# Attention on one core: P of half the units transposed by DMA instead of TensorE, scores run further ahead

## The chip, the cores and the metric

The kernel runs on one core of one Trainium2 chip. Such a core has TensorE (PE; matmuls and their weight loads, PEld), VectorE (DVE), ScalarE (ACT), GpSimd (POOL), and SyncE (SP), which here only issues DMAs; sixteen DMA engines serve all queues. The metric is the device time of one execution in microseconds (us), lower is better. The kernel before takes 1212.79 us, the median of three runs (1212.4 to 1214.84).

## The reference

Two attention problems of the same shape, A and B, with their own inputs; their outputs stand side by side.

```python
B, Sq, D = 16, 144, 448          # x: (B, Sq, D), bfloat16
H, Sk, Dh = 16, 512, 256         # k_cache, v_cache: (B, H, Sk, Dh)
q = (x @ wq).reshape(B, Sq, H, Dh).transpose(0, 2, 1, 3)
scores = einsum("bhqd,bhkd->bhqk", q, k_cache) * Dh ** -0.5
p = softmax(scores, axis=-1)
o = einsum("bhqk,bhkd->bhqd", p, v_cache)
out = o.transpose(0, 2, 1, 3).reshape(B, Sq, H * Dh) @ wo
```

In problem B the reference repeats K and V over head groups, but there are as many of them as heads, so nothing is repeated.

## The kernel before, in words

**Units.** One unit U is one (problem, batch, head): 2 x 16 x 16 = 512 units in one long sequence. The 144 query rows of a unit are split into 112 rows (part A, one unit at a time) and 32 rows (part B, four units stacked to 128 rows).

**One pass of the loop** (variable i, one iteration per unit) emits the steps of several units, each ahead of PV by its own lead:

- Q of unit i+15 (`t_q`, L314: 8 matmuls into the one bank qp_ps) and its copy to qt_sb (`t_evac_q`; VectorE L326 or ScalarE L330).
- every eighth iteration the scores of part B of eight units (`t_sb`, L342).
- scores of part A of unit i+5 (`t_sa`, L418: 2 matmuls into one of two banks sa_ps), the row maximum (VectorE, L429), exp into a slot of pa_sb (ScalarE, L440), and one iteration later the reciprocal (L450) and the multiplication by it on POOL (`t_norm`, L458).
- the transpose of the normalized P of unit i+2 (`t_ta`, L471: 4 transposes by TensorE, 112 x 128 each, back into a bank of sa_ps) and its copy to pt_sb (`t_evac_pta`, VectorE, L481). Keys are taken with a stride: chunk c holds keys 4p+c, as V lies in SBUF with four neighbouring keys per partition. So the transposes read pa_sb with a step of four.
- twice in eight iterations the same for part B (`t_tb`, L394, and L403).
- PV of unit i (`t_pv`, L504: 8 matmuls of V against the transposed P) and its copy to the ring (ScalarE, L519 and L521).
- usually one piece of the output projection (`t_op_piece`, L542: 2 matmuls against wo), from a queue of finished 128-row chunks; stores go out on POOL's queue (`t_store`, L571).

**Loads.** All loads are issued on SyncE's queue in one fixed order: K of eight units as one transposing DMA out of HBM (`t_load_k`, L290, 2 MB), V of four units (`t_load_v`, L299, 1 MB), x of four batches (two transposing DMAs, L280 and L281), wq in four pieces (L259, L261) and wo in eight (L269). The list `dma_plan` is sorted by deadline; an entry is emitted once i has come within a lead of the deadline and its slot's last reader has been emitted. K and V have three slots each (NK, NV), x three (NXG).

**Order and waits.** Each engine's program is written in the order in which the loop emits it. The class `_Sched` keeps, for each buffer slot, who wrote and read it, and puts semaphore waits ahead of an instruction (also of a DMA's issue) where its data or its slot come from another engine. An instruction whose wait isn't met holds everything behind it on its engine; a DMA's issue that waits holds SyncE's later issues. Slot counts that matter: pa_sb 5 (NPA), pt_sb 8 (NPT), qt_sb 12 (NQT).

Of the kernel before, what the change touches and what calls it, by code (L numbers as in the profile page):

```python
# [7 lines left out]
AF = mybir.ActivationFunctionType  # L8
# [4 lines left out]
PE, ACT, DVE, POOL, SP = "pe", "act", "dve", "pool", "sp"  # L13
# [109 lines left out]
def bass_concat_heads__mha_block_cached__gqa_block_cached__near_ridge_kernel(  # L123
# [18 lines left out]
    NP = 2  # L142
    Bn, SQ, D = A_x.shape
# [14 lines left out]
    NWG = NWO // WOG  # L158
    NPC = NWO // OPP

    LQ, LS, LT = 15, 5, 2
    LSB = 7
    NK, NV, NXG = 3, 3, 3
    XB = 4 if Bn % 4 == 0 else (2 if Bn % 2 == 0 else 1)
    NQT, NPA, NPB, NPT, NST, NSTB, NOST = 12, 5, 2, 8, 4, 2, 3
    RS = 4
    RC = RS * 128
    OP_DELAY = 2
# [6 lines left out]
    with contextlib.ExitStack() as es:  # L175
# [33 lines left out]
            sem_names.append("v%d" % i)  # L209
        for i in range(NXG):  # L210
            sem_names.append("xt%d" % i)
        for i in range(HG):
            sem_names.append("wq%d" % i)
        for i in range(NWG):
# [219 lines left out]
        def t_exp(U):  # L434
            bank = U % 2
            sl = U % NST
            psl = U % NPA

            def e(a):
                return a.activation(pa_sb[0:QA, psl, :], sa_ps[bank][0:QA, :], AF.Exp,  # L440
                                    bias=stat[0:QA, NEG + sl:NEG + sl + 1], scale=1.0,
                                    accum_out=stat[0:QA, RSUM + sl:RSUM + sl + 1])
            S.add(ACT, e, reads=[(("sap", bank), ("s", U)), (("neg", sl), U)],
                  writes=[(("pa", psl), (U, 0)), (("rsum", sl), U)], banks=["sa%d" % bank], name="ex%d" % U)
# [17 lines left out]

        def t_ta(U):
            psl = U % NPA
            bank = U % 2

            def e(t):
                src = pa_sb[0:QA, psl, :].rearrange("q (p c) -> q c p", c=4)
                ins = None
                for c in range(4):  # L470
                    ins = t.transpose(pta_ps[bank][:, c * 128:c * 128 + QA], src[:, c, :], ident[0:QA, 0:QA])  # L471
                return ins
            S.add(PE, e, reads=[(("pa", psl), (U, 1)), ("ident", 0)], writes=[(("sap", bank), ("t", U))],
                  banks=["sa%d" % bank], name="TA%d" % U)

        def t_evac_pta(U):
            sl = U % NPT
            bank = U % 2

            def e(v):  # L480
                return v.tensor_copy(pt_sb[:, sl, :, 0:QA],  # L481
                                     pta_ps[bank][:, 0:512].rearrange("p (c q) -> p c q", c=4)[:, :, 0:QA])
            S.add(DVE, e, reads=[(("sap", bank), ("t", U))], writes=[(("pta", sl), U)], banks=["sa%d" % bank],
                  name="epta%d" % U)
# [93 lines left out]
        t_ident()  # L578
        dma_plan = []

        def plan(lo, deadline, lead, fn, *args):
            dma_plan.append((deadline, len(dma_plan), lo, lead, fn, args))

        s_min = -LQ - 24
        for XG in range(NXGT):
            pr, j = divmod(XG, Bn // XB)
            u_first = pr * NU + j * XB * H
            dl = u_first - LQ
            if XG >= NXG:
                pr0, j0 = divmod(XG - NXG, Bn // XB)  # L590
                lo = pr0 * NU + (j0 + 1) * XB * H - 1 - LQ + 1
            else:
                lo = s_min
            plan(lo, dl, 40, t_load_x, XG)
        for pr in range(NP):
            for hg in range(HG):
                dl = pr * NU + 4 * hg - LQ
                lo = pr * NU - H + 4 * hg + 3 - LQ + 1 if pr > 0 else s_min
                plan(lo, dl, 10 ** 6, t_load_wq, pr, hg)
        for wg in range(NWG):  # L600
            plan(s_min, H - 4 + 2 * wg, 10 ** 6, t_load_wo, 0, wg)
        for SG in range(NSG):
            dl = 8 * SG - LSB
            lo = 8 * (SG - NK) + 7 - LS + 1 if SG >= NK else s_min
            plan(lo, dl, 12, t_load_k, SG)
        for G in range(NG):
            dl = 4 * G
            lo = 4 * (G - NV) + 3 + 1 if G >= NV else s_min
            plan(lo, dl, 8, t_load_v, G)
        dma_plan.sort(key=lambda t: t[:2])  # L610
        _prev = s_min
        _tmp = []
        for dl, sq, lo, lead, fn, args in dma_plan:
            _prev = max(_prev, lo, dl - lead)
            _tmp.append((_prev, dl, sq, fn, args))
        dma_plan = _tmp

        u_tail0 = NT - H
        pr_l, b_l, _h = unit(NT - 1)
# [32 lines left out]
        while True:  # L652
            while dma_plan and dma_plan[0][0] <= i:
                _sl, _dl, _sq, fn, args = dma_plan.pop(0)
                fn(*args)
            sgi, ph = divmod(i + LSB, 8)
            do_sb = ph == 0 and 0 <= sgi < NSG
            ga, gb = 2 * sgi, 2 * sgi + 1
            ok = 0 <= sgi < NSG
            if ok and ph == 1:  # L660
                t_exp_b(ga)
            if ok and ph == 3:
                t_exp_b(gb)
            if ok and ph == 2:
                t_recip_b(ga)
                t_norm_b(ga)
            if ok and ph == 4:
                t_recip_b(gb)
                t_norm_b(gb)
            while stores and stores[0][1] <= i:  # L670
                t_store(stores.pop(0)[0])
            if do_sb and sgi == 0:
                t_sb(sgi)
            u = i + LQ
            if 0 <= u < NT:
                t_q(u)
                t_evac_q(u)
            if do_sb and sgi > 0:
                t_sb(sgi)
            u = i + LS  # L680
            if 0 <= u < NT:
                t_sa(u)
                t_max(u)
                t_exp(u)
            u = i + LS - 1
            if 0 <= u < NT:
                t_recip(u)
                t_norm(u)
            u = i + LT
            if 0 <= u < NT:  # L690
                t_ta(u)
                t_evac_pta(u)
            if ok and ph == 3:
                t_tb(ga)
                t_evac_ptb(ga)
            if ok and ph == 7:
                t_tb(gb)
                t_evac_ptb(gb)
            if ok and ph == 0:
                t_max_b(ga)  # L700
            if ok and ph == 2:
                t_max_b(gb)
            u = i
            if 0 <= u < NT:
                t_pv(u)
                t_evac_ot(u)
                pr, b, h = unit(u)
                if u >= u_tail0:
                    for r in tail_chunks:
                        if h == 0:  # L710
                            op_first[r], op_last[r] = 0, NWO - 1
                        for dc in range(2):
                            fifo[tail_bank[r]].append((r, 2 * h + dc, i + 1))
                if h == H - 1:
                    g_end = pr * RP + (b + 1) * SQ
                    lo = (pr * RP + b * SQ) // 128
                    for r in range(lo, (g_end - 1) // 128 + 1):
                        r_end = min((r + 1) * 128, pr * RP + Bn * SQ)
                        if g_end >= r_end and r not in tail_bank:
                            queue_chunk(r, i + OP_DELAY)  # L720
            if i >= 0:
                credit += OP_RATE
            if i >= u_tail0 - 14:
                credit += 4.0
            if i >= NT:
                credit += 4 * OPP
            for bank in ("op", "qp"):
                while fifo[bank] and fifo[bank][0][2] <= i and credit >= 1 and (bank == "qp" or i >= op_hold):
                    r, cs = pop_items(bank, i, OPP)
                    credit -= len(cs)  # L730
                    t_op_piece(r, cs, bank)
                    pr = r // NCH
                    if r == last_chunk_of[pr] and pr + 1 < NP:
                        for c in cs:
                            if c % WOG == WOG - 1:
                                t_load_wo(pr + 1, c // WOG)
                    if cs[-1] == op_last[r]:
                        t_evac_op(r, bank, ACT if bank == "op" else DVE)
                        stores.append((r, i + (2 if i < NT else 0)))
                        if bank == "op":  # L740
                            op_hold = i + 2
            if not fifo["op"] and not fifo["qp"]:
                credit = min(credit, 2.0 * OPP)
            i += 1
            if i >= NT and not fifo["op"] and not fifo["qp"] and not dma_plan and not stores:
                break
# [54 lines left out]
```

## Time and profile before

| what | value |
| --- | --- |
| runs | 1212.79 us median (1212.4 to 1214.84) |
| span of the profiled execution | 1210.9 us, 33868 instructions |
| TensorE, weight loads | 97% and 75% of the span |
| VectorE, ScalarE, POOL | 64%, 62%, 56% |
| transposes of part A on TensorE, L471 | 2048 matmuls, 186.5 us busy, mean 213 ns |
| their copies, L481 | 512, 190.5 us busy, mean 372 ns |
| chain that ended last | TensorE 90% (L471: 8%), DMA 6%, VectorE 2% |
| HBM read, written | 148.90 MB, 4.13 MB |
| K load, issue to landing (median) | 15.0 us for A, 15.1 us for B |
| V load, issue to landing (median) | 6.0 and 6.1 us |
| SyncE waiting for TensorE at V's issues (L299 for L542) | 235.3 us in 59 waits |

The profile is one execution. Busy time of TensorE overlaps itself, since a matmul starts before the one ahead of it has ended: distances between starts show what a step costs. SyncE's rows are issues: the time in a row is how long the queue was held, and landing comes later. A stretch's DMA share is the packets' time over sixteen engines, which can be over 1 where packets overlap.

### The profile page before, as it was taken

The numbers are of one execution on the slowest core, as the hardware profiler recorded it, in microseconds if no ns is written. First come the engines' busy times: TensorE is split into PE (matmuls) and PEld (weight loads), VectorE is DVE, ScalarE is ACT, GpSimd is POOL, SyncE is SP. The second block draws the span as 40 slices with busy tenths as digits, with TensorE's granted clock in tenths as the row PEclk, the third lists the DMA queues.
The fourth block names the chain that finished last, engine by engine and source line by source line (L and its number), as shares of the span: only waits on it lengthen the run. The fifth ranks groups of instructions, "written<-read, shape, count | busy, mean of one in ns | idle before, by whom it ended". The sixth has DMA issues, their size and how long they took to land.

```text
span 1210.9 us, 33868 instructions
## 1 busy us (share of the span) xinstructions
PE 1176.6 (97%) x13952; PEld 902.6 (75%) x13952; DVE 770.1 (64%) x2179; ACT 753.9 (62%) x2213; POOL 679.6 (56%) x682
## 2 busy tenths in 40 slices
PE   4998999999999999999999999999999999999997
PEld 3676777777777777777777777777877777777765
DVE  1765666666666666666566666666666666666563
ACT  1655666666666666666566666666666666666553
POOL 0654565565555565565555655655655655655553
PEclk9999999999999999999999999999999999999999
DMA  9999999999999999999999999999999999999971
GB/s 250 296 269 290 246 255 225 242 251 246 245 238 234 228 263 231 239 239 233 278 284 272 278 272 267 247 257 224 245 245 236 226 245 244 244 239 243 223 178 47
DMA packets 627033, 294.15 MB, mean 243 GB/s; under 512 B 548416, under 2 KB 556608, under 8 KB 626880
## 3 DMA queue, kind: packets, MB, share of 16 engines
q1 hardware_dynamic: 625152, 287.85, 102.2%
q0 software_dynamic: 1728, 4.13, 1.2%
q8 instruction: 111, 1.82, 0.6%
q14 instruction: 42, 0.34, 0.1%
HBM read 148.90 MB, written 4.13 MB: 126 GB/s over the span
## 4 chain that ended last, share of the span: by engine, by line
PE 90%; DMA 6%; DVE 2%; SPq 1%; ACT 0%; issue 0%; POOL 0%; ACTq 0%
PE qp_ps L314 20%; PE ot_ps L504 19%; PE sa_ps L418 18%; PE op_ps L542 17%; PE sa_ps L471 8%; PE sb_ps L342 5%; DMA kt_sb<-in_A_k_cache_dram 4%; PE sb_ps L394 2%; DMA kt_sb<-in_B_k_cache_dram 1%; DVE stat L429 1%; DMA wq_sb<-in_A_wq_dram 0%; PE qp_ps L542 0%; SPq L280 0%; DVE qt_sb L326 0%; DVE pt_sb L481 0%
## 5 line engine op out<-in xcount | busy, mean ns | idle before, releaser
L458 POOL TENSOR_TENSOR pa_sb<-pa_sb,stat 112x512 bf16<-112x512 bf16 x512 | 532.7, 1041 | 491.6 <-DVE stat L450 491.4
L440 ACT ACTIVATE pa_sb<-sa_ps,stat 112x512 bf16<-112x512 f32 x512 | 352.0, 688 | 409.6 <-DVE stat L429 408.6
L429 DVE TENSOR_REDUCE stat<-sa_ps 112x1 f32<-112x512 f32 x512 | 353.9, 691 | 324.7 <-PE sa_ps L418 321.4
L314 PEld LDWEIGHTS qp_ps<-xt_sb,wq_sb 128*128 128x128 bf16 x4096 | 290.5, 99 | 93.1 <-issue 11.3
L314 PE MATMUL qp_ps<-xt_sb,wq_sb 128*128 128x144 bf16 x4096 | 344.1, 228 | 16.1 <-DMA wq_sb<-in_A_wq_dram 10.3
L504 PE MATMUL ot_ps<-pt_sb,v_sb 128*128 128x144 bf16 x4096 | 340.9, 226 | 0.0
L418 PE MATMUL sa_ps<-kt_sb,qt_sb 128*112 128x512 bf16 x1024 | 311.1, 385 | 1.0 <-DVE pt_sb L481 0.8
L542 PE MATMUL op_ps<-wo_sb,ring 128*128 128x448 bf16 x1120 | 279.6, 353 | 0.0
L504 PEld LDWEIGHTS ot_ps<-pt_sb,v_sb 128*128 128x128 bf16 x4096 | 269.1, 98 | 0.4
L471 PEld LDWEIGHTS sa_ps<-ident,pa_sb 112*128 112x128 bf16 x2048 | 161.2, 114 | 104.9 <-ACT pa_sb L440 24.8
L519 ACT ACTIVATE ring<-ot_ps 128x288 bf16<-128x288 f32 (+8 forms) x512 | 190.3, 372 | 4.5 <-PE ot_ps L504 4.5
L481 DVE COPY pt_sb<-sa_ps 128x448 bf16<-128x448 bf16 x512 | 190.5, 372 | 2.4 <-PE sa_ps L471 2.4
L471 PE MATMUL sa_ps<-ident,pa_sb 112*128 112x112 bf16 x2048 | 186.5, 213 | 0.1
L326 DVE TENSOR_SCALAR qt_sb<-qp_ps 128x288 bf16<-128x288 f32 x256 | 117.0, 457 | 98.2 <-PE qp_ps L314 97.5
L382 POOL TENSOR_TENSOR pb_sb<-pb_sb,stat 128x512 bf16<-128x512 bf16 x128 | 133.1, 1040 | 27.1 <-DVE stat L374 27.1
L330 ACT ACTIVATE qt_sb<-qp_ps 128x288 bf16<-128x288 f32 x256 | 106.0, 414 | 35.1 <-PE qp_ps L314 33.4
L418 PEld LDWEIGHTS sa_ps<-kt_sb,qt_sb 128*112 128x112 bf16 x1024 | 96.9, 129 | 38.5 <-issue 26.8
L542 PEld LDWEIGHTS op_ps<-wo_sb,ring 128*128 128x128 bf16 x1120 | 95.5, 98 | 28.1 <-issue 0.9
L440 ACT ACTIVATION_READ_ACCUMULATOR pa_sb<-sa_ps,stat 112x1 f32 x512 | 98.9, 193 | 0.0
L354 DVE TENSOR_REDUCE stat<-sb_ps 128x1 f32<-128x512 f32 x128 | 87.1, 680 | 3.6 <-PE sb_ps L342 3.6
L364 ACT ACTIVATE pb_sb<-sb_ps,stat 128x512 bf16<-128x512 f32 x128 | 88.5, 691 | 0.0
L450 DVE RECIPROCAL stat<-stat 112x1 f32<-112x1 f32 x512 | 78.4, 153 | 0.5 <-ACT pa_sb L440 0.5
(23 smaller groups left out, 368.4 us busy)
## 6 DMA issues: line engine op xcount, KB each, us to landing
v_sb<-in_A_v_cache_dram SPq DMA_DIRECT2D x64, 1024.0 KB, 6.0
v_sb<-in_B_v_cache_dram SPq DMA_DIRECT2D x64, 1024.0 KB, 6.1
out_dram<-ost_sb POOLq DMA_DIRECT2D x36, 112.0 KB, 5.1
wo_sb<-in_A_wo_dram SPq DMA_DIRECT2D x8, 448.0 KB, 7.4
wo_sb<-in_B_wo_dram SPq DMA_DIRECT2D x8, 448.0 KB, 5.7
wq_sb<-in_A_wq_dram SPq DMA_DIRECT2D x4, 768.0 KB, 6.2
wq_sb<-in_B_wq_dram SPq DMA_DIRECT2D x4, 768.0 KB, 7.8
wq_sb<-in_A_wq_dram SPq DMA_DIRECT2D x4, 128.0 KB, 6.6
```

The lines of the kernel that those rows point to most:

```text
L314: ins = t.matmul(qp_ps[:, dc * SQ:(dc + 1) * SQ], lhsT=wq_sb[:, kc, c0:c0 + 128], rhs=xt_sb[:, xsl, kc, xo:xo + SQ], start=(kc == 0 and dc ...
L326: return v.tensor_scalar(qt_sb[:, sl, :, :], src, 1.0 / 16.0, None, op0=ALU.mult)
L382: return g.tensor_tensor(pb_sb[:, psl, :], pb_sb[:, psl, :], stat[:, RINVB + sl:RINVB + sl + 1].to_broadcast([128, SK]), op=ALU.mult)
L418: ins = t.matmul(sa_ps[bank][0:QA, :], lhsT=qt_sb[:, U % NQT, dc, 0:QA], rhs=kt_sb[:, ksl, dc, ko:ko + SK], start=(dc == 0), stop=(dc == 1))
L429: return v.tensor_reduce(stat[0:QA, NEG + sl:NEG + sl + 1], sa_ps[bank][0:QA, :], axis=AX.X, op=ALU.max, negate=True)
L440: return a.activation(pa_sb[0:QA, psl, :], sa_ps[bank][0:QA, :], AF.Exp, bias=stat[0:QA, NEG + sl:NEG + sl + 1], scale=1.0, accum_out=stat ...
L458: return g.tensor_tensor(pa_sb[0:QA, psl, :], pa_sb[0:QA, psl, :], stat[0:QA, RINV + sl:RINV + sl + 1].to_broadcast([QA, SK]), op=ALU.mult)
L471: ins = t.transpose(pta_ps[bank][:, c * 128:c * 128 + QA], src[:, c, :], ident[0:QA, 0:QA])
L481: return v.tensor_copy(pt_sb[:, sl, :, 0:QA], pta_ps[bank][:, 0:512].rearrange("p (c q) -> p c q", c=4)[:, :, 0:QA])
L504: ins = t.matmul(ot_ps[ob][:, dc * SQ:(dc + 1) * SQ], lhsT=v_sb[:, vsl, j, c * DH + dc * 128:c * DH + (dc + 1) * 128], rhs=pt_sb[:, sl, c, ...
L519: ins = a.activation(ring[:, 2 * h:2 * h + 2, c0:c0 + n1], src[:, :, 0:n1], AF.Copy)
L542: ins = t.matmul(acc[0:m, 0:D], lhsT=ring[:, c, col0:col0 + m], rhs=wo_sb[:, c, :], start=(c == first), stop=(c == last))
```

## The change

1. P of units U with U % 8 < 4 is transposed by a DMA out of SBUF (`t_dma_pt`), one for four units: source 112 rows x 2048 columns of pa_sb, destination four neighbouring slots of pt_sb. It is issued on SyncE in the order of the loads, planned at i = U0 - 4 for the four units U0 to U0+3. `t_ta` and `t_evac_pta` of those units are left out; the other four of every eight keep them.
2. Scores of part A (with maximum, exp, normalization) run 12 units ahead of PV instead of 5 (LS); pa_sb has 12 slots instead of 5.
3. Exp writes pa_sb with the keys already grouped by chunk: it reads PSUM with a step of four and writes in order, so a unit's 512 columns are four blocks of 128. `t_ta` reads them in order.
4. The bank of `t_ta` becomes (U+1) % 2, as the lead of the scores went from odd to even.
5. `dma_plan` is ordered by hand: each load has an iteration and a rank among those of the same iteration (wq 0, x and the new DMA 1, K 2, V 3, wo 4). K is planned at 8 SG - 28, V at 4 G - 8.
6. x has two slots instead of three (NXG); two semaphores (pt0, pt1) are added.

```diff
--- before.py
+++ after.py
@@ -158,11 +158,11 @@
     NWG = NWO // WOG
     NPC = NWO // OPP
 
-    LQ, LS, LT = 15, 5, 2
+    LQ, LS, LT = 15, 12, 2
     LSB = 7
-    NK, NV, NXG = 3, 3, 3
+    NK, NV, NXG = 3, 3, 2
     XB = 4 if Bn % 4 == 0 else (2 if Bn % 2 == 0 else 1)
-    NQT, NPA, NPB, NPT, NST, NSTB, NOST = 12, 5, 2, 8, 4, 2, 3
+    NQT, NPA, NPB, NPT, NST, NSTB, NOST = 12, 12, 2, 8, 4, 2, 3
     RS = 4
     RC = RS * 128
     OP_DELAY = 2
@@ -209,6 +209,8 @@
             sem_names.append("v%d" % i)
         for i in range(NXG):
             sem_names.append("xt%d" % i)
+        for i in range(2):
+            sem_names.append("pt%d" % i)
         for i in range(HG):
             sem_names.append("wq%d" % i)
         for i in range(NWG):
@@ -437,7 +439,8 @@
             psl = U % NPA
 
             def e(a):
-                return a.activation(pa_sb[0:QA, psl, :], sa_ps[bank][0:QA, :], AF.Exp,
+                return a.activation(pa_sb[0:QA, psl, :].rearrange("q (c p) -> q c p", c=4),
+                                    sa_ps[bank][0:QA, :].rearrange("q (p c) -> q c p", c=4), AF.Exp,
                                     bias=stat[0:QA, NEG + sl:NEG + sl + 1], scale=1.0,
                                     accum_out=stat[0:QA, RSUM + sl:RSUM + sl + 1])
             S.add(ACT, e, reads=[(("sap", bank), ("s", U)), (("neg", sl), U)],
@@ -462,10 +465,10 @@
 
         def t_ta(U):
             psl = U % NPA
-            bank = U % 2
+            bank = (U + 1) % 2
 
             def e(t):
-                src = pa_sb[0:QA, psl, :].rearrange("q (p c) -> q c p", c=4)
+                src = pa_sb[0:QA, psl, :].rearrange("q (c p) -> q c p", c=4)
                 ins = None
                 for c in range(4):
                     ins = t.transpose(pta_ps[bank][:, c * 128:c * 128 + QA], src[:, c, :], ident[0:QA, 0:QA])
@@ -473,9 +476,23 @@
             S.add(PE, e, reads=[(("pa", psl), (U, 1)), ("ident", 0)], writes=[(("sap", bank), ("t", U))],
                   banks=["sa%d" % bank], name="TA%d" % U)
 
+        def by_dma(U):
+            return U % 8 < 4
+
+        def t_dma_pt(U0):
+            ps0, ts0 = U0 % NPA, U0 % NPT
+            sem = "pt%d" % ((U0 // 8) % 2)
+
+            def e(q):
+                return q.dma_start_transpose(
+                    pt_sb[:, ts0:ts0 + 4, :, :].rearrange("p s c q -> p (s c) q")[:, :, 0:QA],
+                    pa_sb[0:QA, ps0:ps0 + 4, :].rearrange("q s k -> q (s k)")).then_inc(sems[sem], 16)
+            S.add(SP, e, reads=[(("pa", (U0 + j) % NPA), (U0 + j, 1)) for j in range(4)],
+                  writes=[(("pta", (U0 + j) % NPT), U0 + j) for j in range(4)], dma_sem=sem, name="DT%d" % U0)
+
         def t_evac_pta(U):
             sl = U % NPT
-            bank = U % 2
+            bank = (U + 1) % 2
 
             def e(v):
                 return v.tensor_copy(pt_sb[:, sl, :, 0:QA],
@@ -578,42 +595,29 @@
         t_ident()
         dma_plan = []
 
-        def plan(lo, deadline, lead, fn, *args):
-            dma_plan.append((deadline, len(dma_plan), lo, lead, fn, args))
+        def plan(t, prio, fn, *args):
+            dma_plan.append((t, prio, len(dma_plan), fn, args))
 
         s_min = -LQ - 24
         for XG in range(NXGT):
             pr, j = divmod(XG, Bn // XB)
             u_first = pr * NU + j * XB * H
-            dl = u_first - LQ
-            if XG >= NXG:
-                pr0, j0 = divmod(XG - NXG, Bn // XB)
-                lo = pr0 * NU + (j0 + 1) * XB * H - 1 - LQ + 1
-            else:
-                lo = s_min
-            plan(lo, dl, 40, t_load_x, XG)
-        for pr in range(NP):
-            for hg in range(HG):
-                dl = pr * NU + 4 * hg - LQ
-                lo = pr * NU - H + 4 * hg + 3 - LQ + 1 if pr > 0 else s_min
-                plan(lo, dl, 10 ** 6, t_load_wq, pr, hg)
+            lo = u_first - XB * H - LQ + 4 if XG >= NXG else s_min
+            plan(max(lo, u_first - LQ - 40), 1, t_load_x, XG)
+        for hg in range(HG):
+            plan((-32, -29, -26, -21)[hg], 0, t_load_wq, 0, hg)
+            for pr in range(1, NP):
+                plan(pr * NU - H + 4 * hg + 3 - LQ + 1, 0, t_load_wq, pr, hg)
         for wg in range(NWG):
-            plan(s_min, H - 4 + 2 * wg, 10 ** 6, t_load_wo, 0, wg)
+            plan(H - 18 + 2 * wg, 4, t_load_wo, 0, wg)
         for SG in range(NSG):
-            dl = 8 * SG - LSB
-            lo = 8 * (SG - NK) + 7 - LS + 1 if SG >= NK else s_min
-            plan(lo, dl, 12, t_load_k, SG)
+            plan(8 * SG - 28, 2, t_load_k, SG)
         for G in range(NG):
-            dl = 4 * G
-            lo = 4 * (G - NV) + 3 + 1 if G >= NV else s_min
-            plan(lo, dl, 8, t_load_v, G)
-        dma_plan.sort(key=lambda t: t[:2])
-        _prev = s_min
-        _tmp = []
-        for dl, sq, lo, lead, fn, args in dma_plan:
-            _prev = max(_prev, lo, dl - lead)
-            _tmp.append((_prev, dl, sq, fn, args))
-        dma_plan = _tmp
+            plan(4 * G - 8, 3, t_load_v, G)
+        for U0 in range(0, NT, 8):
+            plan(U0 - 4, 1, t_dma_pt, U0)
+        dma_plan.sort(key=lambda t: t[:3])
+        dma_plan = [(t, p, n, fn, args) for t, p, n, fn, args in dma_plan]
 
         u_tail0 = NT - H
         pr_l, b_l, _h = unit(NT - 1)
@@ -687,7 +691,7 @@
                 t_recip(u)
                 t_norm(u)
             u = i + LT
-            if 0 <= u < NT:
+            if 0 <= u < NT and not by_dma(u):
                 t_ta(u)
                 t_evac_pta(u)
             if ok and ph == 3:
```

## Prediction

> **What bounds the kernel now.** I read the engine shares first.
>
> ```profile
> PE 1176.6 (97%) x13952; PEld 902.6 (75%) x13952; DVE 770.1 (64%) x2179; ACT 753.9 (62%) x2213; POOL 679.6 (56%) x682
> ...
> DMA  9999999999999999999999999999999999999971
> ...
> q1 hardware_dynamic: 625152, 287.85, 102.2%
> ```
>
> TensorE leads, but the DMA engines show nine tenths in nearly every slice: two candidates stand close together. The PE timeline in a settled stretch (start, length, line) prices the removed step.
>
> ```profile
> 601.06 0.66 PE L314 MATMUL qp_ps<-xt_sb,wq_sb 128*128 128x144 bf16 x8
> 601.56 0.59 PE L418 MATMUL sa_ps<-kt_sb,qt_sb 128*112 128x512 bf16 x2
> 602.00 0.36 PE L471 MATMUL sa_ps<-ident,pa_sb 112*128 112x112 bf16 x4
> 602.19 0.67 PE L504 MATMUL ot_ps<-pt_sb,v_sb 128*128 128x144 bf16 x8
> 602.70 0.54 PE L542 MATMUL op_ps<-wo_sb,ring 128*128 128x448 bf16 x2
> 603.07 0.66 PE L314 MATMUL qp_ps<-xt_sb,wq_sb 128*128 128x144 bf16 x8
> ```
>
> Lengths overlap; starts don't. Four transposes move the next start by 602.19 - 602.00 = 0.19 us, of a 2.01 us iteration. Next, how full the DMA engines are, by stretch; the last two figures of a row are the DMA share and GB/s.
>
> ```profile
> 38.00:125.00 87.00, 80.80 (x989) 61.41 (x986) 55.81 (x160) 53.33 (x151) 48.73 (x48) 1.00 1.17 279
> 125.00:550.00 425.00, 424.69 (x5111) 327.37 (x5109) 281.26 (x798) 275.14 (x812) 247.77 (x247) 1.00 1.04 242
> 550.00:720.00 170.00, 167.17 (x1986) 129.10 (x1984) 109.81 (x312) 108.19 (x329) 97.07 (x97) 0.99 1.16 274
> 720.00:1150.00 430.00, 429.87 (x5150) 333.31 (x5148) 282.45 (x803) 278.04 (x816) 251.14 (x250) 1.00 1.06 241
> ...
> 388.00:392.00 4.00, 4.00 (x45) 2.88 (x43) 3.34 (x10) 3.66 (x12) 3.03 (x4) 1.00 1.27 290
> 384.00:386.00 2.00, 2.00 (x30) 1.06 (x27) 0.62 (x2) 1.45 (x4) 1.04 (x1) 1.00 1.01 353
> ```
>
> While K streams (388 to 392, a transpose) the engines deliver 290 GB/s at share 1.27; while V streams (384 to 386) 353 at 1.01. Each is full at its own figure; a full mix shows 1.16 to 1.17, as in the first 125 us and around the change of problem (550 to 720). Elsewhere 1.04 and 1.06 leave spare time: 425 x (1 - 1.04/1.165) = 46 us and 430 x (1 - 1.06/1.165) = 39 us, together 85 us. That is all the room a new transfer has before 1150. Last, SyncE's queue where it is fed without a wait.
>
> ```profile
> 93.70 15.29 SPq L290 DMA_TRANSPOSE kt_sb<-in_A_k_cache_dram  x1
> 109.03 1.13 SPq L299 DMA_DIRECT2D v_sb<-in_A_v_cache_dram  x2
> 110.21 14.96 SPq L290 DMA_TRANSPOSE kt_sb<-in_A_k_cache_dram  x1
> ...
> 605.57 15.41 SPq L290 DMA_TRANSPOSE kt_sb<-in_B_k_cache_dram  x1
> 621.03 1.13 SPq L299 DMA_DIRECT2D v_sb<-in_B_v_cache_dram  x2
> 622.20 14.22 SPq L290 DMA_TRANSPOSE kt_sb<-in_B_k_cache_dram  x1
> ```
>
> One K load and two V loads, the food of eight units, take 16.5 us (93.70 to 110.21) and 16.6 us (605.57 to 622.20) of the DMA engines' full attention. TensorE takes 18.1 us for eight units (K issues at 1076.00, 1094.03, 1112.21). So TensorE bounds, with 1.5 us of DMA slack per eight units, out of which x, wq, wo and the stores also live.
>
> **Removed.** 256 of 512 units lose their four transposes: 256 x 0.19 = 48.6 us of TensorE, 0.76 per eight units, so 18.1 becomes 17.35. Their copies out of PSUM (L481, 256 x 372 ns = 95 us of VectorE) were hidden behind TensorE: the kernel's whole wait of L418 for L481 is some 3 us. I count nothing for them.
>
> **Added.** 64 transposes out of SBUF, each 112 x 2048 x 2 bytes = 0.459 MB, on SyncE's queue. No row has a transpose with an SBUF source. The nearest is x's (L280, 0.442 MB): at 0.81 us, with nothing else moving, it held the queue 1.59 us, which scaled is 1.65; K's 290 GB/s gives 1.58; stretched like the fed cycle (16.5 over 7.2 + 5.9 us that bytes and rates give, 1.26) 2.0. From below I bound it by V's 353 GB/s, 1.3 us; from above by L280's longest hold in traffic, 5.5 us. I take 1.7, the row that is the same size. 62 of them fall before the last K load: 105 us against 85 us of room.
>
> The Trainium skill says, in Advanced Engine Details and Errata, X-Bar Transpose (TRN2), that transposing DMAs are as fast as ordinary ones at 350 to 400 GB/s; the K row's 290 against V's 353 differs. An estimate by that page is 1.2 us each, 75 us in all, which the room would hold, and TensorE's saving would be kept. VectorE: DVE Perf Modes, The three transpose paths, speaks against the change: 1309 ns for a 128 x 128 block by DMA against 390 by TensorE. Sixteen blocks would be 21 us, an estimate of some 1300 us over the run; but K's 64 blocks in 7.2 us show 113 ns each when streamed, so I don't use it.
>
> **The sum.** Per eight units the DMA engines need 16.5 + 1.7 = 18.2 us, over TensorE's new 17.35 and over today's 18.1, before x and weights. Over the run: 105 - 85 = +20 us on the path. After the last K load (28 units from the end) the DMA is idle enough, and 14 skipped transposes give 2.7 us back. 1210.9 + 20 - 3 = 1228 us of span; the median of the runs lies 1.9 above the profiled execution, and a balanced pair loses a little to each other, 1 us: **1231 us**.
>
> **Moved and re-ordered.** Each new DMA waits for PV of U0-5 (its pt slots) and for the POOL normalization of U0+3; behind it in SyncE's order stand a K and a V load, and PV of U0 waits for it, as does ACT's exp of U0+12 (the pa slot). From PV of U0-5 to PV of U0 lie four iterations and the front of a fifth, 9.8 us; L280 lands in 4.3 us alone, 8.1 at the median. So no stall of its own, unless the queue is behind. The V load issued after K is the tighter one: new transfer 1.7, K 10.6 (16.5 less 5.9 for two V's), V 3 and 2.8 us of start and landing (L281 lands 3.3 us after its issue, 0.5 of it data) make 18.1 us, against 18.7 us until PV of U0+4 wants it; later than that, it is V that stops TensorE. Scores 12 ahead move K's first need forward and V0 behind K0, K1, K2: three holds of 13 us put V0's issue near 47 us and the first PV near 55, against 37.9 now. Seven more scores and one more 32-row group (7 x 0.44 + 1 us) are then done, so TensorE alone loses 13 us there; in a DMA-bound run this is inside the sum, as the bytes are the same. wq2 and wq3 now stand behind K0 in the queue, 13 us later, near 20 us; Q of unit 8 wants wq2 only after five iterations that themselves wait for K0 (landing near 21 us), so nothing, at worst 2 us. x has two slots instead of three: its load is due 40 units (some 87 us) ahead of first use, when its slot has long been read, far over its 8.1 us. Stores and POOL's queue stay where they are. Exp now reads PSUM with a step of four: ACT is busy 62%, so hidden. The nearest pair, weights read with that step (L471, 113 ns) and without (L504, 98), bounds it between 0 and 15%, 110 ns, which at worst lengthens L471's 25 us of waits for ACT by about 10 us. I take 0.
>
> **Rivals.** (1) The DMA engines absorb it: fed time shrinks below 16.5, or the new transfer costs 1.3, 81 us, within the room. Then TensorE sets the end: 1210.9 - 48.6 + 13 to 30 of start-up = 1175 to 1192; 1185 us, faster (30, if the start is fed as slowly as now: V1 stands behind K3 and V3 behind K4, so the 13th PV comes near 90 us where 62 would be today's). For: the byte rates alone need 13.1 + 1.6 = 14.7 of 17.35 us. Against: no stretch of the trace runs three loads at those rates. (2) The SBUF source is dear: at 3.4 us, the median hold of L280, 62 x 3.4 - 85 = +126 and about 1335 us; it decides from 2.3 us on. Against: the idle L280. (3) Gain and loss cancel, 1213 us.
>
> **How the numbers follow.** DMA-bound at 1.4 to 2.2 us a transfer, 1216 to 1262: 0.52. Dear: 0.16. Absorbed: 0.25. Within 0.2%, about what a measurement of this kernel can tell from no change: 0.07. Both signs hold much, so the whole range is 1190 to 1295, from rival 1 to a transfer of 2.7 us. Faster 0.25, same 0.07, slower 0.68.
>
> **What would show it.** PE share below 95% with K, V or the new transfer as releasers of L504; a DMA share near 1.16 in all stretches up to the last K; K issues 18 to 19 us apart without SyncE waits; L471 at x1024 and still 0.19 a step; first PV near 55 us. I am wrong if K issues come 17.4 us apart with TensorE unbroken (rival 1), or if the new issue holds the queue over 2.3 us (rival 2).

## The result, and the profile after

The changed kernel takes 1245.41 us (median of 4 runs, 1243.59 to 1248.24) against 1213.82 us for the kernel before in the same comparison: a ratio of 1.0261, 95% interval 1.0243 to 1.0279. It is slower by 2.6%. The profiled execution has a span of 1243.7 us, 32.8 above that of before.

The page of the changed kernel: busy time by engine, then the slices for TensorE, its granted clock and the DMA engines, then the chain that ended last.

```profile
span 1243.7 us, 31687 instructions
...
PE 1145.4 (92%) x12928; PEld 858.0 (69%) x12928; DVE 697.9 (56%) x1923; ACT 754.9 (61%) x2213; POOL 679.9 (55%) x682
...
PE   4578899899998999989889988998999999999997
...
PEclk9888999999999999999999999998999999999999
DMA  9999999999999999999999999999999999999962
...
PE 64%; SPq 19%; DMA 13%; ACT 1%; issue 1%; DVE 1%; POOL 0%; ACTq 0%
```

TensorE's busy time fell by 31 us, but its idle time rose from 34 to 98 us, and the chain that was TensorE for 90% is now SyncE's queue and the DMAs for a third. The slices in which TensorE is least busy lie at the start; slices a little below nine tenths are scattered up to two thirds of the run.

The same stretches as before the change (window and length, busy time of PE, PEld, DVE, ACT and POOL, then granted clock, DMA share and GB/s):

```profile
38.00:125.00 87.00, 65.08 (x701) 48.31 (x699) 40.16 (x113) 42.74 (x119) 39.27 (x39) 0.88 1.14 274
125.00:550.00 425.00, 404.07 (x4658) 304.68 (x4657) 253.23 (x700) 273.54 (x806) 248.06 (x247) 0.99 1.17 265
550.00:720.00 170.00, 156.65 (x1744) 117.16 (x1743) 91.79 (x253) 100.37 (x300) 88.83 (x88) 0.96 1.14 273
720.00:1150.00 430.00, 415.75 (x4770) 314.55 (x4768) 257.97 (x713) 278.48 (x826) 251.96 (x251) 0.98 1.15 269
```

The long stretches that showed 1.04 and 1.06 now show 1.17 and 1.15, the figure of a full mix: the room is used up there. Who TensorE waited for at PV (total us, times, longest):

```profile
PE ot_ps L521 <- issue: 21.7, 7, 6.7
...
PE ot_ps L521 <- DMA v_sb<-in_A_v_cache_dram: 20.2, 13, 4.3
...
PE ot_ps L521 <- DMA v_sb<-in_B_v_cache_dram: 16.5, 9, 4.8
...
PE ot_ps L521 <- DMA pt_sb<-pa_sb: 7.0, 1, 7.0
...
PE ot_ps L521 <- ACT qt_sb L332: 2.3, 5, 0.8
```

PV waits 36.7 us for V, each time at the fifth of eight units (two V loads serve eight). The waits put down to "issue" and to ACT are all at the first of eight units, and each ends 0.09 us after the new DMA landed: with the one by name, PV waits 31 us for the transposed P, nearly as long. The longest of these are 7.0 us at unit 0 and 6.7 at unit 16. SyncE's queue shows why V is late (start, how long the queue was held):

```profile
399.93 6.74 SPq L487 DMA_TRANSPOSE pt_sb<-pa_sb  x1
406.71 9.57 SPq L292 DMA_TRANSPOSE kt_sb<-in_A_k_cache_dram  x1
416.32 1.13 SPq L301 DMA_DIRECT2D v_sb<-in_A_v_cache_dram  x2
421.81 3.02 SPq L487 DMA_TRANSPOSE pt_sb<-pa_sb  x1
```

New transfer, K, two V's, new transfer. Between 417.45 and 421.81 SyncE stands before the next new transfer, which waits for PV; the DMA engines are busy with the two V's meanwhile (294 GB/s, share 0.91). That picture, and a chain with K's issue (L292) on it for 18%, suggests a loop through SyncE's order. The experiments show that it is not what sets the time.

Where the time went, by the start of PV of a few units in each profiled execution (us; the second kernel is described below):

| kernel | unit 0 | unit 16 | unit 224 | unit 304 | unit 496 | end |
| --- | --- | --- | --- | --- | --- | --- |
| before | 37.9 | 69.5 | 546.4 | 732.6 | 1168.6 | 1210.9 |
| all P on TensorE, rest as changed | 48.5 | 86.8 | 565.6 | 750.2 | 1186.0 | 1225.0 |
| changed | 50.3 | 98.1 | 575.8 | 776.6 | 1205.8 | 1243.7 |

The changed kernel loses 28.6 us by unit 16, 0.9 from there to unit 224, 14.6 around the change of problem (224 to 304), and gains 6.8 from there to unit 496 and 4.4 to the end.

### The profile page after: what moved, and what is told of

Read it like the earlier page. It is cut to its first block, busy times and chain, and to the rows that moved or that the text cites. A ratio compares the mean times of both kernels' runs of the same rounds, so it can differ in the third digit from the quotient of the medians.

```text
span 1243.7 us, 31687 instructions
## 1 busy us (share of the span) xinstructions
PE 1145.4 (92%) x12928; PEld 858.0 (69%) x12928; DVE 697.9 (56%) x1923; ACT 754.9 (61%) x2213; POOL 679.9 (55%) x682
## 4 chain that ended last, share of the span: by engine, by line
PE 64%; SPq 19%; DMA 13%; ACT 1%; issue 1%; DVE 1%; POOL 0%; ACTq 0%
SPq L292 18%; PE ot_ps L521 15%; PE qp_ps L316 14%; PE op_ps L559 13%; PE sa_ps L420 13%; DMA v_sb<-in_A_v_cache_dram 7%; DMA v_sb<-in_B_v_cache_dram 4%; PE sb_ps L344 3%; PE sa_ps L474 3%; PE sb_ps L396 1%; DMA kt_sb<-in_A_k_cache_dram 1%; DVE stat L431 1%; ACT pa_sb L442 1%; DMA pt_sb<-pa_sb 1%; SPq L487 0%
## 5 line engine op out<-in xcount | busy, mean ns | idle before, releaser
L521 PE MATMUL ot_ps<-pt_sb,v_sb 128*128 128x144 bf16 x4096 | 345.7, 228 | 67.9 <-issue 21.7
L316 PE MATMUL qp_ps<-xt_sb,wq_sb 128*128 128x144 bf16 x4096 | 349.3, 230 | 15.9 <-DMA wq_sb<-in_A_wq_dram 11.3
L316 PEld LDWEIGHTS qp_ps<-xt_sb,wq_sb 128*128 128x128 bf16 x4096 | 295.1, 100 | 98.2 <-issue 15.0
L521 PEld LDWEIGHTS ot_ps<-pt_sb,v_sb 128*128 128x128 bf16 x4096 | 280.5, 99 | 113.2 <-issue 23.2
L559 PE MATMUL op_ps<-wo_sb,ring 128*128 128x448 bf16 x1120 | 282.9, 357 | 0.0
L559 PEld LDWEIGHTS op_ps<-wo_sb,ring 128*128 128x128 bf16 x1120 | 96.2, 99 | 28.6 <-issue 1.8
L474 PEld LDWEIGHTS sa_ps<-ident,pa_sb 112*128 112x128 bf16 x1024 | 72.3, 98 | 61.2 <-ACT pa_sb L442 23.0
L498 DVE COPY pt_sb<-sa_ps 128x448 bf16<-128x448 bf16 x256 | 95.5, 373 | 6.4 <-PE sa_ps L474 6.4
L474 PE MATMUL sa_ps<-ident,pa_sb 112*128 112x112 bf16 x1024 | 93.9, 214 | 1.3 <-ACT pa_sb L442 1.0
```

Source lines behind the costliest of these rows:

```text
L316: ins = t.matmul(qp_ps[:, dc * SQ:(dc + 1) * SQ], lhsT=wq_sb[:, kc, c0:c0 + 128], rhs=xt_sb[:, xsl, kc, xo:xo + SQ], start=(kc == 0 and dc ...
L521: ins = t.matmul(ot_ps[ob][:, dc * SQ:(dc + 1) * SQ], lhsT=v_sb[:, vsl, j, c * DH + dc * 128:c * DH + (dc + 1) * 128], rhs=pt_sb[:, sl, c, ...
L559: ins = t.matmul(acc[0:m, 0:D], lhsT=ring[:, c, col0:col0 + m], rhs=wo_sb[:, c, :], start=(c == first), stop=(c == last))
```

## The experiments

| run | us, median | ratio to before, 95% interval |
| --- | --- | --- |
| V ahead of K (e1) | 1290.76 | 1.0624, 1.0595 to 1.0653 |
| all P on TensorE (e2) | 1225.96 | 1.0094, 1.0075 to 1.0112 |
| K planned later (e3) | 1240.81 | 1.0205, 1.0165 to 1.0245 |
| no wait for PV at the new DMA (e4) | 1247.37 | 1.0277, 1.0256 to 1.0298 |
| two of eight units (e5) | 1213.32 | 0.9992, 0.9981 to 1.0004 |
| changed, K left out (e6) | 1161.2 | 0.956, 0.9539 to 0.9581 |
| before, K left out (e7) | 1204.08 | 0.9913, 0.9892 to 0.9934 |
| two of eight, small lead (e8) | 1208.75 | 0.995, 0.9935 to 0.9964 |
| two and three of eight, none where DMA is full (e9) | 1202.46 | 0.9894, 0.9873 to 0.9915 |
| changed, none where DMA is full (e10) | 1220.15 | 1.0051, 1.0032 to 1.0069 |
| e9, fewer in the second half (e11) | 1198.28 | 0.9877, 0.9859 to 0.9896 |
| V ahead of K and the new DMA early (e12) | 1290.27 | 1.0628, 1.0599 to 1.0657 |

**Is it the order on SyncE's queue?** Two kernels break the supposed loop at different places. The first puts V ahead of K:

```diff
-            plan(8 * SG - 28, 2, t_load_k, SG)
+            plan(8 * SG - 28, 3, t_load_k, SG)
-            plan(4 * G - 8, 3, t_load_v, G)
+            plan(4 * G - 8, 2, t_load_v, G)
```

> Theory F (the DMA engines are full from the first load to the last K, so only bytes ahead of the last K and the work left behind it count): the order of V and K inside a period changes nothing; 1240 to 1250 us, VectorE and TensorE waits on V turn into waits on K or P. Rival O (SyncE's order: PV of U0-5, new DMA, K, V, PV of U0+4 is a loop of some 18 us, longer than TensorE's 17.4): with V ahead of K the loop is 10 us shorter, the period falls to 17.4 and the time to 1205 to 1215 us.

Measured 1290.76 us, 45 us over the changed kernel: both theories missed, F by 41 us and O by 76. The second lets the new DMA go early:

```diff
-    NQT, NPA, NPB, NPT, NST, NSTB, NOST = 12, 12, 2, 8, 4, 2, 3
+    NQT, NPA, NPB, NPT, NST, NSTB, NOST = 9, 12, 2, 12, 4, 2, 2
-            plan(U0 - 4, 1, t_dma_pt, U0)
+            plan(U0 - 6, 1, t_dma_pt, U0)
```

(The constant ones for the identity were put into a slot of pb_sb to make room.)

> pt_sb has 12 slots, so the new DMA waits for PV of U0-9 and SyncE finds the wait met (qt_sb 9 and ost_sb 2 slots make the room). SyncE's some 420 us of waits ahead of the new DMA shrink to under 100. Theory F: the DMA engines were full during those waits, so 1238 to 1250 us. Rival O: K and V are no longer held behind the wait; period 17.4 to 17.7, 1205 to 1225 us.

Measured 1247.37 us, the changed kernel's time and inside theory F's range. SyncE's waits did go: its issues now follow one another without a gap (start, how long held):

```profile
413.59 1.13 SPq L300 DMA_DIRECT2D v_sb<-in_A_v_cache_dram  x2
414.76 6.40 SPq L486 DMA_TRANSPOSE pt_sb<-pa_sb  x1
421.21 9.66 SPq L291 DMA_TRANSPOSE kt_sb<-in_A_k_cache_dram  x1
```

In the timelines the gaps ahead of the new DMA add up to 6 us over the run, against 209 in the changed kernel (the forecast's 420 came from the list of waits). What was a gap became a longer hold: at the median the new DMA now holds the queue for 6.84 us instead of 3.07. (That list still puts 240.9 us of L486 down to POOL here; the timeline has no such gaps, so SyncE didn't wait that long.) So a wait ahead of a DMA's issue cost nothing here: the DMA engines still had work queued. With the waits gone and no microsecond gained, rival O falls. The DMA engines were as full as in the changed kernel; this kernel's row from unit 16 to unit 496 is

```profile
95.90:1210.90 1115.00, 1061.91 (x12096) 798.93 (x12097) 650.45 (x1797) 703.41 (x2080) 633.94 (x632) 0.98 1.16 265
```

against the changed kernel's

```profile
98.10:1205.80 1107.70, 1058.80 (x12097) 797.59 (x12098) 650.69 (x1798) 704.91 (x2080) 635.06 (x632) 0.98 1.15 266
```

**Why did V ahead of K cost 45 us?** Its row between the same units:

```profile
99.40:1250.00 1150.60, 1066.24 (x12096) 800.50 (x12097) 650.43 (x1797) 705.48 (x2080) 633.84 (x632) 0.97 1.16 256
```

The DMA engines are as full (1.16) but deliver 256 GB/s instead of 266. New DMA, V, K, V has four changes between transposing and plain streams per eight units; new DMA, K, V, V has two. The other reading, that the new DMA lands too late behind V (PV waited 58.8 us for it here), was tried by joining the two edits:

> V ahead of K, as in the run that took 1291 us, and the new DMA early, as in the run that took 1247 us (12 slots of pt_sb). Theory T (the DMA engines lose time at each change between transposing and plain streams, and V between the new DMA and K adds two changes to every eight units): still 1283 to 1300 us. Rival L (the new DMA landed late behind V, and PV waited for it): cured by the early issue, 1240 to 1252 us.

Measured 1290.27 us, inside theory T's range. Yet this is no test of rival L, as the new DMA was not issued earlier: at the median 9.0 us ahead of its PV, as with V ahead of K alone, and PV still waited for it (63.3 us by name, 58.8 there). The queue left no room for an earlier issue; its rows follow one another without a gap:

```profile
413.90 4.97 SPq L486 DMA_TRANSPOSE pt_sb<-pa_sb  x1
418.92 0.58 SPq L300 DMA_DIRECT2D v_sb<-in_A_v_cache_dram  x1
419.54 11.03 SPq L291 DMA_TRANSPOSE kt_sb<-in_A_k_cache_dram  x1
```

What the run does show: this kernel and the one with the new DMA early (1247.37 us) differ in the order of K and V alone, both feed the queue almost without gaps (28 and 30 us over the run), and the order makes 43 us. Late landing is then what a slower queue looks like from TensorE. The extra time of V ahead of K is (1250.0 - 99.4 - 1107.7) / 60 = 0.72 us per eight units, 0.36 for each of the two added changes of stream if these are what costs. That is theory T, which fits; no run separates it from another effect of the order, and how the time is lost was not measured.

**What is the new DMA's share, what the rest of the edit's?**

```diff
 def by_dma(U):
-            return U % 8 < 4
+            return False
```

and the calls of `t_dma_pt` are not planned.

> No P goes by DMA, all else as in the changed kernel (lead of 12, order of loads, exp's layout). Theory F: TensorE bounds again at 18.1 us per eight units, but the start keeps its cost, since K0, K1, K2 stand ahead of the first V: first PV near 50 us, 1228 to 1238 us. Rival P (the whole loss is the new DMA's bytes or waits, the rest of the edit is free): 1211 to 1216 us, as before the change.

Measured 1225.96 us, between the two forecasts. So the rest of the edit (above all the lead of 12 and the new order of loads, which no run takes apart) costs 0.94%, 11 us, with no transfer added. Its table row has 17.3 us lost by unit 16, and 14.1 at the end. The new DMA adds 1245.41 - 1225.96 = 19.5 us, TensorE's saving already taken off. By the table the loss lies at the start (11.3 - 1.8 = 9.5 between units 0 and 16) and around the change of problem (26.4 - 10.2 = 16.2); from unit 304 the changed kernel gains 6.6 up to unit 496 on this one.

Is TensorE's saving real? K is the largest load; without it the DMA engines have room:

```diff
-        for SG in range(NSG):
+        for SG in range(NK):
             plan(8 * SG - 28, 2, t_load_k, SG)
```

The kernel before gets the same edit, and in both the scores no longer wait for the loads left out; all later groups use the first three groups' K.

> The changed kernel loads K for the first three groups of eight units only and uses these over and over (the other K loads are left out). Theory F: with the DMA engines idle a third of the time the whole saving of TensorE appears: 1226 less 48.6 is 1177, a little less as x and weights no longer queue: 1168 to 1180 us. Rival O or N (order or number of DMAs): the new DMA still holds SyncE and V behind it, over 1195 us.

> The kernel before with K loaded for the first three groups only (the other K loads are left out). Both theories: TensorE bounds it as it did, only waits for K near the start and the change of problem go: 1200 to 1211 us. Against the changed kernel without K, theory F expects some 30 us more (48.6 saved there, 17 lost at its start).

Measured 1161.2 and 1204.08 us: with room, the change gains 42.9 us in spite of its start, more than the 30 of theory F, and the first time lies 7 us under its range. From unit 16 to unit 496 the gain is 49.3 us, so TensorE's saving (48.6 forecast) is there in full; by unit 16, 11.5 us had been lost. The first also shows the new DMA alone: how long its issue held the queue (ns, minimum, median, maximum) and its landing.

```profile
L487 SPq DMA_TRANSPOSE pt_sb<-pa_sb x64: 1510/1529/4758, 44.1 to 1133.5; - x64
...
DMA to landing us min/median/max: 4.0/4.0/7.3
```

The same lines of the changed kernel, in full traffic:

```profile
L487 SPq DMA_TRANSPOSE pt_sb<-pa_sb x64: 1518/3074/10902, 43.0 to 1217.0; - x64
...
DMA to landing us min/median/max: 4.0/6.2/13.6
```

The hold is not the transfer. Without K, SyncE issues one at 401.64 us; its packets move only from 402.81 to 405.15 us (the last two figures are DMA share and GB/s):

```profile
402.80:405.15 2.35, 2.35 (x33) 1.96 (x32) 1.61 (x6) 2.15 (x8) 1.38 (x3) 1.00 1.09 199
```

Alone the new DMA takes the engines 2.35 us from its first packet to its last, also at the median of all: 0.459 MB at 195 GB/s, where K's stream had 290. As the hold is the shorter of the two, the engines set its pace, not its issue. In traffic its price can be estimated against the kernel with all P on TensorE:

```profile
86.80:1186.00 1099.20, 1090.20 (x13060) 835.07 (x13059) 719.18 (x2041) 704.70 (x2082) 635.19 (x633) 1.00 1.00 244
```

Share times length is 1099 there and 1107.7 x 1.15 = 1274 in the changed kernel; 175 more over 60 new DMAs is 2.9 each, and at K's 1.27 for a transposing stream some 2.3 us, an estimate that agrees with the 2.35.

**Bytes or number?** One DMA for two of eight units instead of four:

```diff
-            return U % 8 < 4
+            return U % 8 < 2
...
-                    pa_sb[0:QA, ps0:ps0 + 4, :].rearrange("q s k -> q (s k)")).then_inc(sems[sem], 16)
+                    pa_sb[0:QA, ps0:ps0 + 2, :].rearrange("q s k -> q (s k)")).then_inc(sems[sem], 16)
```

> P of two of every eight units goes by DMA, one DMA for two units, so half the bytes in as many DMAs. Theory F (bytes on full DMA engines): the need per eight units falls by 0.8 us and fits beside TensorE, which saves 0.38 us per eight units against the kernel with all P on TensorE (1226 us): 1204 to 1214 us. Rival N (each new DMA costs a fixed stop of the stream, whatever its size): the loss of the changed kernel stays, 1238 to 1250 us.

Measured 1213.32 us, no difference from the kernel before: as many DMAs with half the bytes lose 32 us less, though they save TensorE only half as much. So rival N falls. The period between units 304 and 496 is 17.78 us, TensorE's 18.16 less 2 x 0.19.

**Is the price paid only where the DMA engines were already full?**

```diff
+        def n_dma(U):
+            if U < 40 or 224 <= U < 296:
+                return 0
+            return 4
```

> The changed kernel with P of all units on TensorE where the kernel before already fills the DMA engines: units under 40 and 224 to 295 (14 of 64 new DMAs are left to TensorE). Theory F: nearly the whole price of the new DMA (1245 against 1226 with all P on TensorE) is paid in these stretches, 11 us in the first and 16 in the second: 1216 to 1222 us. Rival E (the price is spread evenly over the 64 DMAs): 14 of 64 of 19 us, 1239 to 1243 us.

Measured 1220.15 us, inside theory F's range: leaving out 14 of the 64 transfers took 25 us off. But the price isn't paid there alone. The other 50 spare TensorE 50 x 0.76 = 38 us, and of these only 1225.96 - 1220.15 = 5.8 us arrive. From unit 40 to 224 eight units take 18.06 us, the same as with all P on TensorE; from 304 to 496 they take 17.68 against 18.16. Four of eight fill the other stretches too (DMA share 1.17 from 125 to 550 us).

**Planning K later:**

```diff
-            plan(8 * SG - 28, 2, t_load_k, SG)
+            plan(8 * SG - 20 if SG else -28, 2, t_load_k, SG)
```

> K of a group is planned 20 units ahead of its first unit, not 28 (the first one stays). Theory F: the last K leaves 8 units later, 28 in place of 36 units are left behind it, and the DMA engines work beside 8 units (17 us) more of TensorE: 1226 to 1232 us. Rival O: the loop is untouched, only the start gains some microseconds: 1236 to 1243 us.

Measured 1240.81 us (the interval allows 1235.9 to 1245.7): some 5 us, by the intervals between none and 10, not the 17 of theory F. It lies in rival O's range, whose point here, that only the start gains, needs no loop. The first PV came at 43.2 instead of 50.3 us, and unit 16 at 90.2 instead of 98.1; by unit 496 it stood at 1204.9 against 1205.8. The last K left at 1181.4 instead of 1163.0, with the V loads and the new DMA of eight more units now ahead of it. So "bytes ahead of the last K" was the wrong bound: a load moved back lets others move forward, and full engines stay full. Where exactly the start's gain was lost again stays open.

**A faster kernel.** Three versions put this together: fewer units by DMA, scores 8 ahead (pa_sb 10 or 12 slots), K 20 ahead, the first V ahead of the second K.

> Two of eight units by DMA, scores only 8 units ahead, K planned 20 ahead, the first V ahead of the second K. Theory F: the start costs only a few microseconds over the kernel before, the DMA need fits, and TensorE saves 24 us: 1188 to 1198 us, faster than both kernels. Rival: if the lead isn't what costs the start, 1204 to 1214 as the kernel with two of eight and a lead of 12.

Measured 1208.75 us, short of the forecast and inside the rival's range. The start did gain (first PV at 41.2 us, against 50.5 with a lead of 12), but PV of unit 16 came at 86.8, after 6.6 us of waiting for a new DMA that was issued behind x's load and wo's. The next one leaves the full stretches alone and plans wo and x later:

```diff
+            if U < 40 or 224 <= U < 296:
+                return 0
+            return 3 if (U // 8) % 2 else 2
...
-            plan(H - 18 + 2 * wg, 4, t_load_wo, 0, wg)
+            plan(H - 10 + 2 * wg, 4, t_load_wo, 0, wg)
```

> The new DMA only where the DMA engines have room (none under unit 40 and from 224 to 295, else two and three units of eight in turn), scores 8 ahead, K 20 ahead, first V ahead of the second K, wo and x planned later. Theory F: the start and the change of problem cost what they cost before, and 50 groups save 2.5 x 0.19 us each: 1213 less 24 plus a few, 1188 to 1196 us. Rival E: not under 1203 us.

Measured 1202.46 us, 6 us short of theory F and half a microsecond under rival E's bound, with three of six runs above it: it decides nothing between them. Its period from unit 304 was 17.98 us, longer than the 17.75 with two of eight (but e10, with four of eight, had 17.68 there, so the number of units alone doesn't set it):

> The last version with two of eight units instead of two and three in turn from unit 296 on, and wo planned 4 iterations earlier. Theory F: from unit 304 to 496 the period goes back from 17.98 to the 17.75 us that two of eight showed, 5 us, and TensorE's wait for wo near 90 us (6.6 us) shrinks: 1192 to 1199 us. If the limit there isn't the DMA engines: no change, 1200 to 1205 us.

Measured 1198.28 us, ratio 0.9877 (0.9859 to 0.9896): 1.2% faster than the kernel before and 47 us faster than the change as made. The period from unit 304 went to 17.75 us, as forecast, but the intervals of this run and of e9 overlap, so it is not shown that the last step gained. Its page:

```profile
PE 1155.1 (97%) x13504; PEld 873.8 (73%) x13504; DVE 737.4 (62%) x2067; ACT 754.0 (63%) x2213; POOL 678.6 (57%) x682
...
PE   4889999999999999999989999999999999999997
```

TensorE is nearly unbroken again, with 21.5 us less to do than before the change (1176.6 to 1155.1).

## Why the prediction was right, and where it wasn't

The forecast was slower, by DMA engines that become the bound, at 1231 us; 1245.41 came out, inside that case's own 1216 to 1262 (by the same sum 1.4 us a transfer gives 1213, not 1216). The direction and the cause, too little room on the DMA engines, were right; the loss, 31.6 us, is nearly twice the one forecast. Point by point:

- **0.19 us per skipped group of transposes**: right. Without K loads the period between units 304 and 496 is 17.34 us, against 18.16 for the kernel before without K: 0.82 per eight units, 0.76 forecast. So the skipped copies and exp's new reading order gained and cost next to nothing, as taken:

```profile
L442 ACT ACTIVATE pa_sb<-sa_ps,stat 112x512 bf16<-112x512 f32 x512 | 352.2, 688 | 394.2 <-DVE stat L431 364.8
...
L474 PEld LDWEIGHTS sa_ps<-ident,pa_sb 112*128 112x128 bf16 x1024 | 72.3, 98 | 61.2 <-ACT pa_sb L442 23.0
```

Exp stays at 688 ns with a step of four in PSUM. The weight loads that now read in order fall from 113 to 98 ns.
- **1.7 us per new transfer**: the term that was mis-sized. The row of the same size gave how long the issue held the queue (1.59 us; the new one 1.53 alone), and that is not how long the engines work. Alone they took 2.35 us. The profile before had it: the packets of x's two loads (0.59 MB) move from 2.19 to 5.26 us of the kernel before, which is 2.4 us for the new transfer's bytes.
- **105 us against 85 us of room, so 20 us lost**: the new DMA cost 19.5 us net of TensorE's saving, but that the two agree is luck. With 2.35 us each the same sum gives 62 x 2.35 - 85 = 61 us. The room was not 85 us either: by the same rule the kernel with all P on TensorE has 1099 x (1 - 1.00/1.165) = 156 us of it. And the sum pooled the room of the whole run, while room in one stretch is of no use to another: 14 transfers in full stretches carried 25 us, and elsewhere four of eight ate most of what TensorE saved (e10).
- **"In a DMA-bound run this is inside the sum"**: the other step that failed. The later first PV was taken as free, but the changed kernel is 28.6 us behind by unit 16 and gets 11 us back after unit 304. The kernel with all P on TensorE loses 11 us without any new transfer. With the transfer's 19.5 that makes 30.5 of the 31.6 us between the two medians (the kernel before had 1213.82 in one comparison and 1214.89 in the other); the sum had 17. How much of the 11 the changed kernel still pays is not shown: K later brought its first PV 7.1 us forward, and little of that reached the end.
- **"After the last K load (28 units from the end)"**: a slip. K is planned 28 units ahead of its group's first unit, which leaves 36 units, with 61 new DMAs ahead of it instead of 62. K 8 units later gained about 5 us, so it explains little of the miss.
- **The V load behind K is what stops TensorE first**: right as a wait (36.7 us, against 31 for the new DMA), and no cause: with V first, PV no longer waited for V, and the time rose.
- **The dear source** (rival 2, from 2.3 us): its sign came, as the new issue held the queue for 3.07 us at the median, and 2.35 us alone lies just over its border. Yet the time is far from its 1335. The sign "without SyncE waits" didn't come: 209 us of gaps stand ahead of the new DMA. **Absorbed** (rival 1): seen in full only where K was left out.

The Trainium skill's page VectorE: DVE Perf Modes, The three transpose paths, gives 1309 ns for a block of 128 x 128. That doesn't hold for a streamed transfer out of SBUF: 14 full blocks' worth of data (0.459 MB) in 2.35 us is 168 ns each (4.0 us from issue to landing).

## What to carry to other kernels

Before work is moved to the DMA engines, look at their share stretch by stretch, and compare it with the share of a stretch known to be full: a mean hides that the start and a change of weights have no room. Move only as much as fits there; two or three of eight units away from the full stretches, with a shorter lead and later loads, gained 1.2%; four of eight everywhere lost 2.6%. Price a transfer by when its packets move, not by how long its issue holds the queue. Count a longer lead as a cost of its own: here the loads that it needs earlier stood ahead of the first product.

## What the runs showed of the hardware that was not expected

- The order new DMA, V, K, V (four changes between transposing and plain streams per eight units) took 0.72 us more than new DMA, K, V, V (two), with the DMA share all but unchanged (1.16 and 1.15) and 256 GB/s instead of 266.
- A transposing DMA out of SBUF moved 0.459 MB in 2.35 us with the engines otherwise idle, 195 GB/s, while its issue held the queue for 1.53 us.
- After a long wait TensorE runs slower for a while. The changed kernel's first PV, after 7 us of waiting, took 1.14 us for its eight matmuls:

```profile
50.34 1.14 PE L521 MATMUL ot_ps<-pt_sb,v_sb 128*128 128x144 bf16 x8 [7.01 <-DMA pt_sb<-pa_sb]
```

The kernel before, without that wait:

```profile
37.86 0.66 PE L504 MATMUL ot_ps<-pt_sb,v_sb 128*128 128x144 bf16 x8
```

The Trainium skill's page TensorE: Matmul & The Clock Gate, Why this matters for your kernels, warns of idle gaps over some 3 us; the row agrees. PV of unit 5 (64.68 us) took 1.17 us too, after a wait of only 2.46 us ahead of unit 4. The granted clock of that stretch, 38 to 125 us, is 0.88 against 1.00 before the change (0.91 with all P on TensorE). So part of the start's loss can be the slower clock that follows the waits; no run separates it.
